# Fewer matmuls around the output projection of a cached decode step, and output weights of three head groups loaded in unequal parts

## The chip, the cores and the metric

The kernel runs on one core of one Trainium2 chip. The metric is the device time in microseconds (us) of one execution; a run gives the median of several. The inputs and the output are float32.

## The reference

Two attention blocks A and B read the same small input `x` (2 batches, 512 columns), each with its own key and value caches (2 batches, 32 heads, 4096 tokens, 128 per head) and weights, and a sigmoid gate mixes the two results. Cut to what matters:

```python
x = A_x                                              # (2, 1, 512)
g = sigmoid((x * gate_w).sum(-1, keepdims=True))
def block(x, k_cache, v_cache, wq, wo):
    q = (x @ wq).reshape(B, 1, 32, 128)               # one query row per batch and head
    scores = einsum("bhqd,bhkd->bhqk", q, k_cache) * 128 ** -0.5
    o = einsum("bhqk,bhkd->bhqd", softmax(scores), v_cache)
    return o.reshape(B, 1, 32 * 128) @ wo             # (2, 1, 512)
return g * block(A) + (1 - g) * block(B)
```

Each cache value is used once, so 570 MB come in from HBM and 4 KB go out.

## The kernel before, in words

A *group* is four heads of one network (8 groups in each of A and B); a *unit* `u` is a group and a batch, so there are 32 units, and two units in a row (b = 0 and 1) share a group. Each quarter of the 128 partitions holds one head of the unit, and each partition 128 tokens.

For a unit the keys come in two tiles of 4 MB (`kt`, three buffers), the values in one tile of 8 MB (`vt`, one buffer). For each group there is one tile of output weights (`wo`, 1 MB, two buffers): 128 rows of 8 KB, one for each partition. VectorE (DVE) multiplies the keys by the query and sums along the head (`scores`, L252 and L254), then finds the maximum (`soft`). ScalarE (ACT) makes the exponentials. TensorE (PE) multiplies them with the values (`values`, L275, 32 matmuls of 512 columns into four strips of 32 rows of one PSUM tile `vp`); ACT copies `vp` to `vs`; PE gathers the four heads (`gather_out`), DVE divides by the sums and applies the gate (`normalise`), PE deals the result over the partitions (`spread_out`, L326) and multiplies it with the output weights into `acc` (`project_out`, L336). A float32 matmul of the code stands twice in the trace as a weight load and a matmul.

The order is written out by hand: every engine runs its own instructions in the order of the code, and a loop over `u` works on the keys of unit u, the values of unit u - 1 and the output of the group that ended before that. All large loads are issued by SyncE (SP) from one queue, in the order of the list `order`; `pump` takes the next one as soon as the tile that it overwrites has been used. SP runs them in that order, so a load that waits holds back all loads behind it. Eight semaphores go round over the loads, so a load also waits for the one that had its semaphore before. The last unit's values come in pieces that get smaller (`load_v_half`), and the last group's output weights come last of all, in two pieces.

Of the kernel before, what the change touches and what calls it, by code (L numbers as in the profile page):

```python
# [13 lines left out]
P = 128  # L14
B = 2
# [11 lines left out]
KB = 3  # L27
VC = 4
NVC = NS // VC
NPR = 3  # L30
QT = 32
STRIPS = P // QT
OR = G * DH // P
EC = D // STRIPS
SCALE = DH ** -0.5
QUARTERS = [slice(j * PH, (j + 1) * PH) for j in range(G)]


@with_exitstack
def tile_gated_decode(ctx: ExitStack, tc: tile.TileContext, ins: dict, out: bass.AP):  # L40
# [52 lines left out]
    def load_wo(n, g):  # L93
        wo[n, g] = wpool.tile([P, OR, D], F32, name="wo")
        rows = ins[n + "_wo"][g * G * DH:(g + 1) * G * DH]
        if (n, g) != last:
            nc.sync.dma_start(wo[n, g], rows.rearrange("(p r) e -> p r e", p=P))
        else:

            t = rows.rearrange("(h p) e -> p h e", p=P)  # L100
            for i in range(0, G, 2):
                nc.sync.dma_start(wo[n, g][:, i:i + 2], t[:, i:i + 2])
# [35 lines left out]
    pump()  # L138


    consts.tile([P, 32], F32, name="gap")
    ident = consts.tile([P, P], F32)
    make_identity(nc, ident)
    ones = consts.tile([P, P], F32)
# [3 lines left out]
    for c in range(KC):  # L148
# [5 lines left out]
    nc.vector.memset(xs, 0.0)  # L154
    nc.vector.tensor_copy(xs[:, :, :B], cols_ps[:, :, :B])

    one = consts.tile([P, STRIPS, B, PH], F32)
    nc.vector.tensor_copy(
        one, ident.rearrange("p (s q) -> p s q", q=QT)[:, :, :B, None].to_broadcast([P, STRIPS, B, PH]))

    padded, sums, sums_of_values = [], [], []
    for i in range(NPR):
        t = consts.tile([P, NVC, G * VC], F32, name=f"pr{i}")
        nc.vector.memset(t, 0.0)
        padded.append(t)
    for i in range(2):
        t = ps.tile([P, VC * DH], F32, name=f"vp{i}", bufs=1)
        nc.vector.memset(t, 0.0)  # L170
        sums_of_values.append(t)

    outs = []
    for i in range(2):
        t = consts.tile([P, OR, QT], F32, name=f"on{i}")
        nc.vector.memset(t, 0.0)
        outs.append(t)
# [6 lines left out]
    pick = consts.tile([P, VC, G], F32)  # L184
    nc.vector.tensor_reduce(
        pick, ident.rearrange("p (s j a) -> p a j s", s=STRIPS, a=VC)[:, :, :G, :], axis=AX.X, op=ALU.add)

    picks = consts.tile([P, B, VC, B, G], F32)
    nc.vector.memset(picks, 0.0)
    for b in range(B):  # L190
        nc.vector.tensor_copy(picks[:, b, :, b, :], pick)

    qa, qrow = {}, {}

# [14 lines left out]
    def spread_queries(u):  # L209

        n, g, b = units[u]
        qp = ps.tile([P, DH], F32, name="qp", bufs=1)
        for j, quarter in enumerate(QUARTERS):
            nc.tensor.matmul(qp[quarter], one[:, g % STRIPS, b], qrow[n][:, g // STRIPS, j * DH:(j + 1) * DH],  # L214
                             start=True, stop=True)
        qs[u] = work.tile([P, DH], F32, name="q", bufs=3)
        nc.scalar.activation(qs[u], qp, AF.Copy)  # L217


    gate = {}  # L220
# [1 line left out]
    def make_gate():  # L222
# [12 lines left out]
        gate["last"] = consts.tile([P, B, G], F32, name="gate")  # L235
        nc.vector.tensor_copy(gate["last"], other[:, :, None].to_broadcast([P, B, G]))
        mine = consts.tile([B * G, B], F32, name="mine")
        nc.vector.tensor_reduce(mine, ident[:B * G, :B * G].rearrange("p (b h) -> p b h", b=B), axis=AX.X, op=ALU.add)
        for n, t in (("A", g), ("B", other)):
            m = consts.tile([B * G, B], F32, name="gm" + n)  # L240
            nc.vector.tensor_tensor(m, mine, t[:B * G], op=ALU.mult)
            gate[n] = consts.tile([B * G, 1], F32, name="gate" + n)
            nc.vector.tensor_reduce(gate[n], m, axis=AX.X, op=ALU.add)

    sc, pr, lp, vp, ot, ls, vs, on, rs, row, cp = ({} for _ in range(11))

    def scores(u, i, k):

# [7 lines left out]
    def soft(u):  # L256
        rm = work.tile([P, 1], F32, name="rm")
        nc.vector.tensor_reduce(rm, sc[u], axis=AX.X, op=ALU.max)  # L258

        across = work.tile([P, PH], F32, name="across")  # L260
        nc.vector.transpose(across, rm.to_broadcast([P, PH]))
        nm = work.tile([P, 1], F32, name="nm")
        nc.vector.tensor_reduce(nm, across, axis=AX.X, op=ALU.max, negate=True)  # L263
        n, g, b = units[u]
        pr[u], lp[u] = padded[u % NPR], sums[u // B % 3]
        for j, h in enumerate(QUARTERS):
            nc.scalar.activation(pr[u][h, :, j * VC:(j + 1) * VC], sc[u][h].rearrange("p (c a) -> p c a", a=VC),  # L267
                                 AF.Exp, bias=nm[h], accum_out=lp[u][h, b * G + j:b * G + j + 1])

    def values(u):  # L270
        vp[u] = sums_of_values[u % 2]
        for c in range(NVC):
            s = c % STRIPS
            t = vt[u][:, c * VC:(c + 1) * VC] if u in vt else vt[u, c * VC // NT][:, c * VC % NT:c * VC % NT + VC]
            nc.tensor.matmul(vp[u][s * QT:s * QT + G * VC], pr[u][:, c, :], t.rearrange("p a d -> p (a d)"),  # L275
                             start=c < STRIPS, stop=c >= NVC - STRIPS)
        vs[u] = work.tile([P, VC * DH], F32, name="vs")
        nc.scalar.activation(vs[u], vp[u], AF.Copy)  # L278

    def gather_out(u):  # L280
        n, g, b = units[u]
        if (n, g) == last:

            if b == 0:
                ot[n, g] = ps.tile([P, B, G], F32, name="ot", bufs=1)
            for a in range(VC):
                nc.tensor.matmul(ot[n, g][:, b], vs[u][:, a * DH:(a + 1) * DH], pick[:, a],  # L287
                                 start=a == 0, stop=a == VC - 1)
            return
        if b == 0:  # L290
            ot[n, g] = ps.tile([B * G, DH], F32, name="ot", bufs=1)
        for a in range(VC):
            nc.tensor.matmul(ot[n, g], picks[:, b, a].rearrange("p b j -> p (b j)"), vs[u][:, a * DH:(a + 1) * DH],  # L293
                             start=(b, a) == (0, 0), stop=(b, a) == (B - 1, VC - 1))

    def sum_of(n, g, u):

        if (n, g) == last:
            ls[n, g] = ps.tile([P, B * G], F32, name="small", bufs=1)
            nc.tensor.matmul(ls[n, g], ones, lp[u], start=True, stop=True)  # L300
        else:
            ls[n, g] = ps.tile([B * G, 1], F32, name="small", bufs=1)
            nc.tensor.matmul(ls[n, g], lp[u], ones[:, :1], start=True, stop=True)  # L303

    def invert(n, g):
        rs[n, g] = work.tile(ls[n, g].shape, F32, name="rsl" if (n, g) == last else "rs", bufs=1)
        nc.vector.reciprocal(rs[n, g], ls[n, g])
        by = gate["last"].rearrange("p b h -> p (b h)") if (n, g) == last else gate[n]
        nc.vector.tensor_tensor(rs[n, g], rs[n, g], by, op=ALU.mult)

    def normalise(n, g):
        on[n, g] = outs[g % 2]
        if (n, g) == last:
            nc.vector.tensor_tensor(on[n, g][:, :, :B].rearrange("d h b -> d b h"), ot[n, g],  # L314
                                    rs[n, g].rearrange("p (b h) -> p b h", b=B), op=ALU.mult)
            return
        row[n, g] = work.tile([B * G, DH], F32, name="row", bufs=1)
        nc.vector.tensor_scalar(row[n, g], ot[n, g], rs[n, g], None, op0=ALU.mult)  # L318

    def spread_out(n, g):  # L320


        cp[n, g] = ps.tile([P, OR, B], F32, name="small", bufs=1)
        for h in range(G):
            for r in range(OR):
                nc.tensor.matmul(cp[n, g][h * QT:(h + 1) * QT, r], row[n, g][:, r::OR], ident[:B * G, h:B * G:G],  # L326
                                 start=True, stop=True)
        nc.scalar.activation(on[n, g][:, :, :B], cp[n, g], AF.Copy)  # L328


    acc = ps.tile([P, EC], F32, name="acc", bufs=1)

    def project_out(n, g):
        for r in range(OR):
            for s in range(STRIPS):
                nc.tensor.matmul(acc[s * QT:(s + 1) * QT], on[n, g][:, r], wo[n, g][:, r, s * EC:(s + 1) * EC],  # L336
                                 start=(n, g, r) == ("A", 0, 0), stop=(n, g, r) == (*last, OR - 1))

    for c in range(KC):
        project("A", c)  # L340
# [5 lines left out]
    for u in range(NU + 2):  # L346
# [7 lines left out]
        if u + 1 < NU:  # L354
            spread_queries(u + 1)
        if ended and ended != last:
            spread_out(*ended)
        if ends:
            sum_of(*ends, v)
        if u < NU:  # L360
            scores(u, 0, 1)
            used("k", u, 0)
        if ends:
            invert(*ends)
        if 0 <= v < NU:
            values(v)
            used("v", v)
            gather_out(v)
        if ended:
            project_out(*ended)  # L370
            used("wo", *ended)
# [40 lines left out]
```

## Time and profile before

| | before |
|---|---|
| median of 3 runs (lowest to highest) | 1331.59 us (1331.37 to 1331.93) |
| profiled execution, its own time | 1331.76 us |
| its span in the profile | 1330.0 us |
| HBM read | 570.43 MB, 429 GB/s over the span |
| busy share of the span: PE, DVE, ACT | 29%, 87%, 7% |
| PE matmuls and weight loads | 3724 and 3724 |

The device time is 1.8 us longer than the span, which runs from the first to the last instruction. In the windows of the profile, PEclk is the clock that TensorE was granted as a share of full speed, and the DMA share is the mean busy share of the core's 16 DMA engines; a packet is counted where it starts, so in short windows the share can be a little over 1. In the list of queues, q1 is the queue of SP's loads, and q8 and q14 are those over which the engines' own instructions are fetched. A row of the chain of waits gives the start in us, the length in us, and what took the time.

### The profile page before, as it was taken

How to read it: one execution, taken by the hardware profiler on the slowest of the kernel's cores; microseconds unless marked ns; L12 is line 12 of the kernel's file. 1: busy time of each engine (PE TensorE's matmuls, PEld its weight loads, DVE VectorE, ACT ScalarE, POOL GpSimd, SP SyncE). 2: the span in 40 equal slices, each digit the busy share in tenths (PEclk: the TensorE clock that was granted, in tenths of full speed). 3: DMA queues.
4: the chain of work that ended last, by engine and by line, in shares of the span. 5: the costliest groups of instructions: out<-in, count | busy, mean ns of one | idle time of the engine just before them, and what ended most of it. 6: DMA issues, size and time to landing. Idle time of an engine off the chain costs nothing.

```text
span 1330.0 us, 8602 instructions
## 1 busy us (share of the span) xinstructions
PE 391.7 (29%) x3724; PEld 136.3 (10%) x3724; DVE 1157.8 (87%) x429; ACT 96.9 (7%) x341; POOL 0.7 (0%) x6
## 2 busy tenths in 40 slices
PE   4033123333213332152123332223332133332136
PEld 1000001101001110010001101011110011100012
DVE  2999999989989898938998989989899998989984
ACT  0000000000000000000000000000000000000000
POOL 0000000000000000000000000000000000000000
PEclk9566566765566666586576665666665566665669
DMA  9999999999999999999999999999999999999997
GB/s 410 442 433 417 438 427 447 428 428 433 432 443 428 436 427 432 431 443 423 437 433 441 428 427 435 432 436 436 436 429 429 432 433 445 434 419 434 429 436 315
DMA packets 18172, 570.99 MB, mean 429 GB/s; under 512 B 1995, under 2 KB 2003, under 8 KB 2774
## 3 DMA queue, kind: packets, MB, share of 16 engines
q1 hardware_dynamic: 18120, 570.44, 99.4%
q8 instruction: 29, 0.48, 0.1%
q14 instruction: 9, 0.07, 0.0%
q10 hardware_dynamic: 14, 0.01, 0.0%
HBM read 570.43 MB, written 0.00 MB: 429 GB/s over the span
## 4 chain that ended last, share of the span: by engine, by line
DMA 75%; PE 21%; DVE 3%; issue 0%; SPq 0%; ACT 0%; ACTq 0%; DVEq 0%
DMA vt<-in_A_v_cache_dram 38%; DMA vt<-in_B_v_cache_dram 30%; PE vp L275 20%; DMA kt<-in_B_k_cache_dram 3%; DMA kt<-in_B_v_cache_dram 2%; DMA kt<-in_A_wq_dram 2%; DVE sc L254 1%; DVE kt L252 1%; PE qa L201 1%; SPq L66 0%; PE acc L336 0%; ACT vs L278 0%; PE ot L287 0%; PE small L225 0%; PE ot L293 0%
## 5 line engine op out<-in xcount | busy, mean ns | idle before, releaser
L252 DVE TENSOR_TENSOR kt<-kt,q 128x4096 f32<-128x4096 f32 x128 | 565.1, 4415 | 120.0 <-DMA kt<-in_A_k_cache_dram 54.2
L254 DVE TENSOR_REDUCE sc<-kt 128x32 f32<-128x4096 f32 x128 | 565.8, 4420 | 4.4
L275 PE MATMUL vp<-vt,pr 128*16 128x512 f32 x1984 | 283.1, 734 | 709.3 <-DMA vt<-in_A_v_cache_dram 380.2
L275 PEld LDWEIGHTS vp<-vt,pr 128*16 128x16 f32 x1984 | 63.3, 113 | 903.7 <-issue 505.5
L278 ACT ACTIVATE vs<-vp 128x512 f32<-128x512 f32 x32 | 19.1, 597 | 961.9 <-PE vp L275 961.9
L326 PE MATMUL small<-ident,row 8*32 8x2 f32 x480 | 21.5, 197 | 160.5 <-DVE row L318 160.5
L267 ACT ACTIVATE pr<-sc,nm 32x128 f32<-32x128 f32 x128 | 51.0, 398 | 63.7 <-DVE nm L263 61.9
L293 PE MATMUL ot<-vs,picks 128*8 128x128 f32 x240 | 31.2, 273 | 23.3 <-ACT vs L278 23.3
L326 PEld LDWEIGHTS small<-ident,row 8*32 8x32 f32 x480 | 20.3, 149 | 164.6 <-DVE row L318 164.6
L293 PEld LDWEIGHTS ot<-vs,picks 128*8 128x8 f32 x240 | 19.1, 89 | 54.4 <-ACT vs L278 50.9
L201 PE MATMUL qa<-kt,xs 128*32 128x512 f32 x128 | 20.3, 787 | 13.1 <-DMA kt<-in_B_wq_dram 4.5
L267 ACT ACTIVATION_READ_ACCUMULATOR pr<-sc,nm 32x1 f32 x128 | 23.5, 184 | 0.0
L336 PE MATMUL acc<-wo,on 128*32 128x128 f32 x512 | 19.6, 275 | 0.3 <-DVE on L314 0.3
L214 PE MATMUL qp<-qrow,one 128*32 128x128 f32 x256 | 18.0, 278 | 0.4 <-ACT q L217 0.4
L336 PEld LDWEIGHTS acc<-wo,on 128*32 128x32 f32 x512 | 15.4, 109 | 0.4 <-DVE on L314 0.4
L229 DVE TENSOR_SCALAR ge<-ge 128x2 f32<-128x2 f32 x1 | 0.2, 169 | 16.4 <-ACT ge L228 16.4
L328 ACT ACTIVATE on<-small 128x8 f32<-128x8 f32 x15 | 2.7, 179 | 157.9 <-PE small L326 157.9
L314 DVE TENSOR_TENSOR on<-ot,rsl 128x8 f32<-128x8 f32 x1 | 0.2, 172 | 12.2 <-PE ot L287 12.2
L217 ACT ACTIVATE q<-qp 128x128 f32<-128x128 f32 x32 | 8.9, 278 | 17.6 <-PE small L303 17.0
L258 DVE TENSOR_REDUCE rm<-sc 128x1 f32<-128x128 f32 x32 | 9.2, 286 | 1.1
L214 PEld LDWEIGHTS qp<-qrow,one 128*32 128x32 f32 x256 | 9.8, 108 | 2.1 <-ACT qrow L207 0.8
L275 PE MATMUL vp<-kt,pr 128*16 128x512 f32 x64 | 8.7, 595 | 2.2 <-DMA kt<-in_B_v_cache_dram 2.2
(50 smaller groups left out, 52.6 us busy)
## 6 DMA issues: line engine op xcount, KB each, us to landing
kt<-in_B_k_cache_dram SPq DMA_DIRECT2D x32, 4096.0 KB, 37.2
kt<-in_A_k_cache_dram SPq DMA_DIRECT2D x31, 4096.0 KB, 34.5
kt<-in_A_wq_dram SPq DMA_DIRECT2D x2, 4096.0 KB, 21.2
wo<-in_A_wo_dram SPq DMA_DIRECT2D x8, 1024.0 KB, 32.0
kt<-in_B_wq_dram SPq DMA_DIRECT2D x2, 4096.0 KB, 35.9
vt<-in_B_v_cache_dram SPq DMA_DIRECT2D x2, 4096.0 KB, 27.2
wo<-in_B_wo_dram SPq DMA_DIRECT2D x7, 1024.0 KB, 31.3
kt<-in_B_v_cache_dram SPq DMA_DIRECT2D x3, 2048.0 KB
```

The costliest lines, as they stand in the source:

```text
L201: nc.tensor.matmul(qa[n, i // STRIPS][s * QT:(s + 1) * QT], xs[:, c], wq[n, c][:, i * G * DH:(i + 1) * G * DH], start=c == 0, stop=c == KC ...
L214: nc.tensor.matmul(qp[quarter], one[:, g % STRIPS, b], qrow[n][:, g // STRIPS, j * DH:(j + 1) * DH], start=True, stop=True)
L217: nc.scalar.activation(qs[u], qp, AF.Copy)
L252: nc.vector.tensor_tensor(t, t, qs[u][:, None, :].to_broadcast([P, NH, DH]), op=ALU.mult)
L254: nc.vector.tensor_reduce(sc[u][:, c:c + NH], t, axis=AX.X, op=ALU.add)
L258: nc.vector.tensor_reduce(rm, sc[u], axis=AX.X, op=ALU.max)
L267: nc.scalar.activation(pr[u][h, :, j * VC:(j + 1) * VC], sc[u][h].rearrange("p (c a) -> p c a", a=VC), AF.Exp, bias=nm[h], accum_out=lp[u] ...
L275: nc.tensor.matmul(vp[u][s * QT:s * QT + G * VC], pr[u][:, c, :], t.rearrange("p a d -> p (a d)"), start=c < STRIPS, stop=c >= NVC - STRIPS)
L278: nc.scalar.activation(vs[u], vp[u], AF.Copy)
L293: nc.tensor.matmul(ot[n, g], picks[:, b, a].rearrange("p b j -> p (b j)"), vs[u][:, a * DH:(a + 1) * DH], start=(b, a) == (0, 0), stop=(b, ...
L326: nc.tensor.matmul(cp[n, g][h * QT:(h + 1) * QT, r], row[n, g][:, r::OR], ident[:B * G, h:B * G:G], start=True, stop=True)
L336: nc.tensor.matmul(acc[s * QT:(s + 1) * QT], on[n, g][:, r], wo[n, g][:, r, s * EC:(s + 1) * EC], start=(n, g, r) == ("A", 0, 0), stop=(n, ...
```

## The change

The change has two parts.

The arithmetic around the values is laid out anew. Both batches of a group go into one `vp`: the exponentials stand in a tile that is zero for the other batch, so a matmul has 32 columns of weights where it had 16, and `vs` and the gather are done once for a group. The gather now gives its result with the head's 128 elements on the partitions (`pick`, 4 matmuls of 8 columns). Dealing it out takes 4 matmuls (`deal_out`) and two DVE operations (`keep_own`) where it took 16 small matmuls and an ACT copy; the projection takes 4 matmuls of 512 columns (into `most`, 2 partitions) where it took 16 of 128 columns; the query is spread by one matmul of 512 columns and four ACT copies where it took four matmuls and one copy. Only the last group keeps the old projection into `acc`; `take_most` adds what the other fifteen gave.

The output weights of groups 4, 5 and 6 of B are loaded in several transfers: the first 112 partitions, and then the last 16 in parts of 8, 8; of 7, 5, 3, 1; and of 6, 4, 4, 2.

```diff
+PARTS = {("B", 4): (112, 120), ("B", 5): (112, 119, 124, 127), ("B", 6): (112, 118, 122, 126)}
...
-            nc.sync.dma_start(wo[n, g], rows.rearrange("(p r) e -> p r e", p=P))
+            src = rows.rearrange("(p r) e -> p r e", p=P)
+            cuts = (0, *PARTS.get((n, g), ()), P)
+            for i, j in zip(cuts, cuts[1:]):
+                nc.sync.dma_start(wo[n, g][i:j], src[i:j])
...
     def spread_queries(u):
-        qp = ps.tile([P, DH], F32, name="qp", bufs=1)
+        qp = ps.tile([P, G, DH], F32, name="qp", bufs=1)
+        k = g % STRIPS * QT + b
+        nc.tensor.matmul(qp, ident[:, k:k + 1].to_broadcast([P, P]), qrow[n][:, g // STRIPS], start=True, stop=True)
...
-            nc.tensor.matmul(qp[quarter], one[:, g % STRIPS, b], qrow[n][:, g // STRIPS, j * DH:(j + 1) * DH],
-                             start=True, stop=True)
-        nc.scalar.activation(qs[u], qp, AF.Copy)
+            nc.scalar.activation(qs[u][quarter], qp[quarter, j], AF.Copy)
...
+    def gather_out(n, g):
+        vs[n, g] = work.tile([P, VC * DH], F32, name="vs", bufs=1)
+        nc.scalar.activation(vs[n, g], vp[n, g], AF.Copy)
+        ot[n, g] = ps.tile([P, B * G], F32, name="small", bufs=1)
+        for a in range(VC):
+            nc.tensor.matmul(ot[n, g], vs[n, g][:, a * DH:(a + 1) * DH], pick[:, a], start=a == 0, stop=a == VC - 1)
...
+    def deal_out(n, g):
+        cp[n, g] = ps.tile([P, OR, B, G], F32, name="small", bufs=1)
+        for r in range(OR):
+            nc.tensor.matmul(cp[n, g][:, r].rearrange("p b h -> p (b h)"), deal[:, r].rearrange("p g q -> p (g q)"),
+                             on[n, g], start=True, stop=True)
+    def keep_own(n, g):
+        t = work.tile([P, OR * B, G], F32, name="all", bufs=1)
+        nc.vector.tensor_tensor(t, cp[n, g].rearrange("p r b h -> p (r b) h"),
+                                own[:, None, :].to_broadcast([P, OR * B, G]), op=ALU.mult)
+        on[n, g] = work.tile([P, OR * B], F32, name="dealt")
+        nc.vector.tensor_reduce(on[n, g], t, axis=AX.X, op=ALU.add)
...
+            if (n, g) != last:
+                nc.tensor.matmul(most, on[n, g][:, r * B:(r + 1) * B], wo[n, g][:, r],
+                                 start=(n, g, r) == ("A", 0, 0), stop=(n, g, r) == ("B", NG - 2, OR - 1))
+                continue
...
+    def take_most():
+        kept = consts.tile([B, D], F32, name="kept")
+        nc.scalar.activation(kept, most, AF.Copy)
+        for s in range(STRIPS):
+            nc.tensor.matmul(acc[s * QT:(s + 1) * QT], ident[:B, :QT], kept[:, s * EC:(s + 1) * EC],
+                             start=True, stop=False)
```

On PE, the rows of one group (from the query of the unit to the projection of the group before; the last number of a row is a count). Before:

```order
L214 MATMUL qp<-qrow,one 32x128 x4
L303 MATMUL small<-ones,lp_121 8x1
L275 MATMUL vp_113<-vt,pr_105 16x512 x32
L293 MATMUL ot<-vs,picks 8x128 x4
L214 MATMUL qp<-qrow,one 32x128 x4
L326 MATMUL small<-ident,row 32x2 x16
L275 MATMUL vp_111<-vt,pr_107 16x512 x32
L293 MATMUL ot<-vs,picks 8x128 x4
L336 MATMUL acc<-wo,on_117 32x128 x16
```

And after:

```order
L208 MATMUL qp<-qrow,ident 128x512
L279 MATMUL small<-lp_111,ones 128x8
L264 MATMUL vp<-vt,pr_105 32x512 x32
L274 MATMUL small<-pick,vs 128x8 x4
L208 MATMUL qp<-qrow,ident 128x512
L300 MATMUL small<-on,deal 128x8 x4
L264 MATMUL vp<-vt,pr_103 32x512 x32
L318 MATMUL most<-wo,dealt 2x512 x4
```

These are 113 matmuls of the code before and 79 after; the matmuls on the values keep their number and place, and the rest shrinks.

On SP, the loads around the output weights of group 5 of B. Before:

```order
L66 DMA vt<-in_B_v_cache_dram 128x16384
L97 DMA wo<-in_B_wo_dram 128x2048
L66 DMA kt<-in_B_k_cache_dram 128x8192 x2
L66 DMA vt<-in_B_v_cache_dram 128x16384
L66 DMA kt<-in_B_k_cache_dram 128x8192 x2
```

And after:

```order
L67 DMA vt<-in_B_v_cache_dram 128x16384
L101 DMA wo<-in_B_wo_dram 112x2048
L101 DMA wo<-in_B_wo_dram 7x2048
L101 DMA wo<-in_B_wo_dram 5x2048
L101 DMA wo<-in_B_wo_dram 3x2048
L101 DMA wo<-in_B_wo_dram 1x2048
L67 DMA kt<-in_B_k_cache_dram 128x8192 x2
L67 DMA vt<-in_B_v_cache_dram 128x16384
L67 DMA kt<-in_B_k_cache_dram 128x8192 x2
```

Five transfers stand where one stood, ahead of the next keys; no load changes its turn.

On PE, the end of the program, from the projection of the last group but one. Before:

```order
L336 MATMUL acc<-wo,on_115 32x128 x16
L300 MATMUL small<-lp_119,ones 128x8
L275 MATMUL vp_113<-kt,pr_107 16x512 x32
L287 MATMUL ot<-pick,vs 128x4 x4
L336 MATMUL acc<-wo,on_117 32x128 x16
```

And after:

```order
L318 MATMUL most<-wo,dealt 2x512 x4
L279 MATMUL small<-lp_109,ones 128x8
L329 MATMUL acc<-kept,ident 32x128 x4
L264 MATMUL vp<-kt,pr_105 32x512 x32
L274 MATMUL small<-pick,vs 128x8 x4
L322 MATMUL acc<-wo,wide 32x128 x16
```

The four matmuls of `take_most` have come in ahead of the last unit's values; what follows the values has the same count.

More of the change, by code (lines that the diff above doesn't have):

```diff
@@ L138, in tile_gated_decode @@
     pump()
-    consts.tile([P, 32], F32, name="gap")
+    consts.tile([P, 104], F32, name="gap")
     ident = consts.tile([P, P], F32)
@@ L155, in tile_gated_decode @@
     nc.vector.tensor_copy(xs[:, :, :B], cols_ps[:, :, :B])
[L157 to L165, printed above, removed]
+    padded, sums = [], []
+    for i in range(B):
+        t = consts.tile([P, NVC, B, G * VC], F32, name=f"pr{i}")
         nc.vector.memset(t, 0.0)
         padded.append(t)
[L168 to L177, printed above, removed]
+    wide = consts.tile([P, G, QT], F32)
+    nc.vector.memset(wide, 0.0)
     for i in range(3):
@@ L233, in make_gate @@
         nc.vector.tensor_scalar(other, g, -1.0, 1.0, op0=ALU.mult, op1=ALU.add)
[L235 to L238, printed above, removed]
         for n, t in (("A", g), ("B", other)):
[L240 to L245, printed above, removed]
+            gate[n] = consts.tile([P, B, G], F32, name="gate" + n)
+            nc.vector.tensor_copy(gate[n], t[:, :, None].to_broadcast([P, B, G]))
+    sc, lp, vp, ot, ls, vs, on, rs, cp = ({} for _ in range(9))
     def scores(u, i, k):
@@ L296, in sum_of @@
[L296 to L309, printed above, removed]
@@ new lines, in sum_of, with invert, normalise @@
+    def sum_of(n, g, u):
+        ls[n, g] = ps.tile([P, B * G], F32, name="small", bufs=1)
+        nc.tensor.matmul(ls[n, g], ones, lp[u], start=True, stop=True)
+    def invert(n, g):
+        rs[n, g] = work.tile([P, B * G], F32, name="rs", bufs=1)
+        nc.vector.reciprocal(rs[n, g], ls[n, g])
+        nc.vector.tensor_tensor(rs[n, g], rs[n, g], gate[n].rearrange("p b h -> p (b h)"), op=ALU.mult)
+    def normalise(n, g):
+        if (n, g) == last:
+            nc.vector.tensor_tensor(wide[:, :, :B].rearrange("d h b -> d b h"),
+                                    ot[n, g].rearrange("p (b h) -> p b h", b=B),
@@ L315, in normalise @@
                                     rs[n, g].rearrange("p (b h) -> p b h", b=B), op=ALU.mult)
             return
[L317 to L328, printed above, removed]
+        on[n, g] = work.tile([P, B * G], F32, name="on", bufs=1)
@@ L331, in tile_gated_decode @@
+    most = ps.tile([B, D], F32, name="most", bufs=1)
     acc = ps.tile([P, EC], F32, name="acc", bufs=1)
@@ L362, in tile_gated_decode @@
             used("k", u, 0)
+        if ended and ended != last:
+            keep_own(*ended)
         if ends:
             invert(*ends)
+        if u == NU:
+            take_most()
         if 0 <= v < NU:
@@ L367, in tile_gated_decode @@
             used("v", v)
-            gather_out(v)
+        if ends:
+            gather_out(*ends)
         if ended:
```

56 lines of the change are left out of this document (20 added, 36 removed).

## The prediction

> **What bounds the kernel now.** I read the page first (busy shares, queues, the chain), then the chain in order of time, then the last microseconds in windows of 1 us.
>
> ```profile
> PE 391.7 (29%) x3724; PEld 136.3 (10%) x3724; DVE 1157.8 (87%) x429; ACT 96.9 (7%) x341; POOL 0.7 (0%) x6
> q1 hardware_dynamic: 18120, 570.44, 99.4%
> q8 instruction: 29, 0.48, 0.1%
> HBM read 570.43 MB, written 0.00 MB: 429 GB/s over the span
> L252 DVE TENSOR_TENSOR kt<-kt,q 128x4096 f32<-128x4096 f32 x128 | 565.1, 4415 | 120.0 <-DMA kt<-in_A_k_cache_dram 54.2
> ```
>
> SP's loads keep the 16 DMA engines busy for 99.4% of the span; the busiest computing engine, DVE, is idle for 120 us ahead of this line alone, 54.2 of them waiting for the keys of A. So the bytes bound the kernel, and a third of the matmuls is off the path as work. What can move the time is how the bytes end.
>
> ```profile
> 1234.10 40.06 DMA kt<-in_B_k_cache_dram
> ...
> 1293.52 29.18 DMA kt<-in_B_v_cache_dram
> 1322.75 1.06 PE vp L275 x4
> ...
> 1327.01 0.29 DVE total L386
> ```
>
> The chain of waits ends in a load: the last piece of values lands at 1322.70 (1293.52 + 29.18), and copy, gather, projection and output follow it to 1330.0.
>
> ```profile
> 1318.00:1319.00 1.00, 1.00 (x12) 0.23 (x8) 0.00 (x0) 0.00 (x0) 0.00 (x0) 1.00 0.98 397
> 1319.00:1320.00 1.00, 0.72 (x8) 0.00 (x0) 0.00 (x0) 0.00 (x0) 0.00 (x0) 1.00 0.67 272
> 1320.00:1321.00 1.00, 0.70 (x8) 0.13 (x8) 0.00 (x0) 0.00 (x0) 0.00 (x0) 1.00 0.59 240
> 1321.00:1322.00 1.00, 0.81 (x8) 0.12 (x4) 0.00 (x0) 0.00 (x0) 0.00 (x0) 1.00 0.60 231
> 1322.00:1323.00 1.00, 0.83 (x6) 0.12 (x4) 0.00 (x0) 0.00 (x0) 0.00 (x0) 1.00 0.53 193
> 1323.00:1324.00 1.00, 0.79 (x4) 0.00 (x0) 0.00 (x0) 0.11 (x1) 0.00 (x0) 1.00 0.39 152
> 1324.00:1325.00 1.00, 0.46 (x4) 0.46 (x5) 0.00 (x0) 0.49 (x1) 0.00 (x0) 1.00 0.23 88
> 1325.00:1326.00 1.00, 0.74 (x11) 0.65 (x14) 0.17 (x1) 0.00 (x0) 0.00 (x0) 1.00 0.00 0
> ```
>
> The last but one column is the DMA share. It doesn't fall at once. Up to 1319 all 16 engines work; then the share is 0.67, so five of them have run out; at 1322 to 1323 about half are left (0.53); after 1325 none. If a load of 128 partitions gives every engine the same bytes, the late engines have had something else to do. From 1319 to 1325 the missing shares sum to 0.33 + 0.41 + 0.40 + 0.47 + 0.61 + 0.77 = 2.99 us. That is what perfect balance would give, and every load's landing waits for the latest engine.
>
> **Where the lateness comes from.**
>
> ```profile
> q8 instruction: 1, 0.02, 0.6%
> q8 instruction: 1, 0.02, 0.3%
> ```
>
> These are from the queue lists of the windows 80 to 90 and 1310 to 1330 us. In the first, one instruction packet took 0.6% of 16 engines x 10 us, 0.96 us of one engine; the second shows that one of the 29 came in the last 20 us. The page has 29 such packets, 0.48 MB; PE ran 3724 + 3724 = 7448 instructions, 257 for each packet, so PE is being fed in blocks. The last half of the engines (0.53 + 0.39 + 0.23 = 1.15 us of 16 engines after 1322, 18.4 engine-us, so 2.3 us each) end at 1324.3 on average, 5.2 us after the first five. If 28 packets went to these eight by turns, 3.5 each, one costs 1.49 us, the packet and a gap about it. If they went over all 16, the step between 1319 and 1322 would not be there. I take 1.4 to 1.5.
>
> [...]
>
> **The change part by part.**
>
> *Fewer PE instructions.* The order gives 1864 matmuls of the code before and 1348 after (16 groups of 79, 72 to project the queries and set up, 12 more in the last group); at four instructions each, 5392, and 5392 / 257 = 21 packets, 20 before the end where there were 28. Over eight engines by turns the latest has three where it had four: 1 x 1.45 = **-1.4 us** on the path. Bounds: 0, if the packets have no part in the lateness; two packets fewer on the latest, -2.9.
>
> *Parts of the output weights.*
>
> ```profile
> wo<-in_B_wo_dram SPq DMA_DIRECT2D x7, 1024.0 KB, 31.3
> ```
>
> A load is 128 rows of 8 KB, 1.05 MB at 429 GB/s = 2.44 us, and eight rows for each engine: 0.306 us a row. 112 partitions are seven rows an engine; the other 16 rows go in parts of at most eight, so on at most eight engines if one row is one piece. An engine that gets none is spared one row in each of three loads: 3 x 0.306 = **-0.9 us**. The first engine gets up to 10 rows (2 + 4 + 4) instead of 3, +2.1 us, and 2.1 us on an engine that ran out at 1319 is covered by the 3.5 us that the latest then still has. No row shows which engines a small part takes. If they are the late ones, it is +2.1 instead. I take -0.9: late and early engines are two halves of eight, and the half that parts are dealt to is one or the other; the range keeps both ends. [...]
>
> The ten more transfers cost SP turns.
>
> ```profile
> 1233.25 0.44 SPq L97
> SPq L102 <- DMA vt<-in_B_v_cache_dram: 8.8, 1, 8.8
> ```
>
> An issue takes 0.44 us, so the next keys go out 0.9 to 1.8 us later; the load above took 31.3 us from issue to landing, 2.4 of them its own, so some 29 us of queue cover it. The 8.8 us show the eight semaphores at work: the last load waited for the one eight before it. With five parts in a row the load eight before is at least a unit's keys old (some 30 us), and has landed. 0.
>
> *The new order of the output.*
>
> ```profile
> L318 DVE TENSOR_SCALAR row<-ot,rs 8x128 f32<-8x128 f32 x15 | 4.9, 329 | 0.0
> 1262.04 8.83 PE L275 MATMUL vp<-vt,pr 128*16 128x512 f32 x64 [26.22 <-DMA vt<-in_B_v_cache_dram]
> ```
>
> DVE gets three operations of 8 or 32 columns for a group where it had one of 128 (L318, 0.33): at most +0.7 us for two units, beside its idle time: 0. `keep_own` waits for four matmuls that are issued a `scores` of 8.8 us (two of 4.4) earlier; without that cover DVE would lose their 1 us a group. The projection grows from 16 matmuls of 128 columns side by side to four of 512 one after the other: at 0.45 us a pass (below) 8 x 0.45 = 3.6 us, behind the values and ahead of the next unit's, for which PE has waited 26.22 us. 0.
>
> At the end the cover is thin:
>
> ```profile
> 1312.93 3.63 PE L275 MATMUL vp<-kt,pr 128*16 128x512 f32 x32
> 1317.81 1.91 PE L275 MATMUL vp<-kt,pr 128*16 128x512 f32 x16 [1.25 <-DMA kt<-in_B_v_cache_dram]
> 1320.30 1.05 PE L275 MATMUL vp<-kt,pr 128*16 128x512 f32 x8 [0.58 <-DMA kt<-in_B_v_cache_dram]
> 1323.89 0.60 ACT L278 ACTIVATE vs<-vp 128x512 f32<-128x512 f32 x1 [11.33 <-PE vp L275]
> ```
>
> 32 matmuls in four strips take 3.63 us, 0.45 for a pass of 512 columns. The last unit's values start at 1312.93 and then wait for loads, 1.25 us and 0.58 us. `take_most` puts an ACT copy of 512 columns (0.60) and four matmuls (at most 0.45) ahead of them, with DVE's 0.7 at most 1.75 us. The two waits together are 1.83. The keys before it land earlier by the same as the values, so the order of the two keeps. 0, up to +0.5. After the last load the counts on PE, ACT and DVE are the same.
>
> *The start.*
>
> ```profile
> 0.74 0.88 SPq L90 DMA_DIRECT2D kt<-in_A_wq_dram  x2
> 27.63 0.43 PE L214 MATMUL qp<-qrow,one 128*32 128x128 f32 x8
> 28.33 0.27 ACT L217 ACTIVATE q<-qp 128x128 f32<-128x128 f32 x1
> 29.07 0.17 ACT L228 ACTIVATE ge<-small 128x2 f32<-128x2 f32 x1 [0.47 <-PE small L225]
> 30.64 4.40 DVE L252 TENSOR_TENSOR kt<-kt,q 128x4096 f32<-128x4096 f32 x1
> 48.31 0.33 SPq L66
> ```
>
> At 48.31 SP issues keys that had waited for DVE's first two scores. Ahead of them stood five tiles of 4.19 MB, 48.9 us at 429 GB/s, issued from 0.74 on and so begun between 1 and 2: the queue was some 2 us from empty. So here the path runs through the first query. Its matmul goes from 0.43 to two passes of 0.45 or more (+0.5), three more copies come in ahead of `ge` on ACT (0.2 to 0.27 each, partly beside PE's work on the gate), and `ge` comes 0.7 us later; the gate loses four small DVE operations of the 1.4 us between `ge` and L252, 0.6. Net **+0.1**, between -0.3 and +0.7.
>
> **The sum.** -1.4 - 0.9 + 0.1 = -2.2 or -2.3 us against the profiled execution's 1331.76 us (span 1330.0): 1329.5. That execution stands 0.17 above the median, so I predict 1329.3 us, -0.17%. About 0.2%, 2.7 us, is what a measurement of this kernel tells from no change, so the forecast falls just inside it.
>
> **The rivals.**
> - *Full balance.* The latest engine loses two packets, or its load falls to the mean: 2.99 us of missing shares and 8 packets x 1.45 / 16 = 0.7 make 3.7 us, 1327.9. For it: five engines idle for 6 us have room for all rows. Against: 20 packets on eight engines leave three on some.
> - *The parts go to the late engines, or to one that is late for another reason* (there are engines that ran out between 1319 and 1322, late by 1 to 3 us without being of the last eight). Then 2.1 us eat the gain: 1329.9 to 1332.4. The rows show no number of an engine.
> [...]
> - *Slower: the parts collide.* All loads of before but a few tiny ones write 128 partitions, eight an engine; a load of 112 may give engines rows that two must write by the same way. If the 16 last rows go four deep (4 x 0.306 instead of 0.306, +0.9) and the seven at half speed (+2.1), three loads cost 9.2 us on every engine: 1331.6 - 1.4 + 9.2 = 1339.4; a quarter of that, 2.3, is the point from which it decides, and 5 us from which it is slower by 0.2%. No row speaks for or against it. [...]
>
> **How the numbers follow.** Main case 0.52, about 1328.4 to 1330.3; full balance 0.14; no gain or little (wrong engines, hidden fetch, tail or start) 0.19; collision 0.15, most of it over 1332. Faster by over 0.2% (under 1328.9): all of full balance and four tenths of the main case, 0.35. Slower by over 0.2% (over 1334.3): 0.12 of the collision. Same: 0.53. The range leaves out what lies under 1328.0 (0.07) and the collisions over 1333.0 (0.13). The main case's own range is 1328.4 to 1330.3.
>
> **What would show it.** Packets on q8: 21. The fall of the DMA share at the end: the missing shares under 2 us, and from full to none in under 4.5 us. The last values landing 2.2 us earlier, near 1320.5, with the same 7.3 us behind. SP's keys of 48.31 within 0.7 us. Wrong would be: a DMA rate that dips near 1262 us (1233.25 and 29 of queue) and one and two groups earlier, where the parts are loaded (collision); a late engine that the tail shows beyond 4.5 us (wrong engines); PE without a wait between the last values' pieces (the tail has become computing).

## The result, and the profile after

The changed kernel takes 1347.40 us (1346.37 to 1352.97) against 1331.59: a ratio of 1.0122 [1.0111, 1.0133], slower by 16 us. The forecast was 1329.3. The profiled execution took 1346.37 us, its span is 1344.6.

On the page after, these rows answer to those shown of before (busy us, share and instructions of PE; then what the DMA engines moved in 40 slices of 33.6 us; then packets, MB and share by queue, and the bytes read):

```profile
PE 452.8 (34%) x2692; PEld 151.0 (11%) x2692; DVE 1159.6 (86%) x449; ACT 110.8 (8%) x407; POOL 0.7 (0%) x6
GB/s 406 437 435 423 435 435 446 431 423 431 435 435 435 436 435 426 431 443 422 436 434 434 438 433 437 423 431 430 438 437 435 424 370 445 433 356 429 369 427 324
q1 hardware_dynamic: 18168, 570.44, 99.5%
q8 instruction: 21, 0.34, 0.1%
HBM read 570.43 MB, written 0.00 MB: 424 GB/s over the span
```

Before, what the DMA engines moved (40 slices of 33.25 us) was:

```profile
GB/s 410 442 433 417 438 427 447 428 428 433 432 443 428 436 427 432 431 443 423 437 433 441 428 427 435 432 436 436 436 429 429 432 433 445 434 419 434 429 436 315
```

PE has 28% fewer matmuls but more busy time, 452.8 us against 391.7, which is still far from the span. The bytes are the same and q1 is as busy as before, but the rate over the span has fallen from 429 to 424 GB/s. The loss isn't spread out: three slices, the 33rd, 36th and 38th, stand at 370, 356 and 369 GB/s, and the others near those of before. The busy share of 99.5% doesn't show it; the windows below have 0.98 at 230 GB/s and 0.96 at 413.

The chain of waits shows the same as time (start, length, what): the start of the values of three units, before

```profile
1062.49 9.66 PE vp L275 x64
1142.26 9.03 PE vp L275 x64
1223.50 9.37 PE vp L275 x64
```

and after, with the last piece of all:

```profile
1061.17 9.79 PE vp L264 x64
1146.93 9.57 PE vp L264 x64
1231.87 9.77 PE vp L264 x64
1337.21 1.08 PE vp L264 x4
```

At 1061 us the changed kernel is 1.3 us ahead. One dip later it is 4.7 behind, then 8.4, and at the last piece (1322.75 before) 14.5. So 15.8 us are lost in three steps of 6.0, 3.7 and 6.1, 5.3 on average.

Windows of 10 us on the first dip, after, and the middle one of before. The columns are the length, then the busy time and the count of PE, of its weight loads, of DVE, ACT and POOL, then PEclk, the DMA share and GB/s:

```profile
1085.00:1095.00 10.00, 0.00 (x0) 0.00 (x0) 9.93 (x5) 0.00 (x0) 0.00 (x0) 0.50 0.97 419
1095.00:1105.00 10.00, 0.28 (x4) 0.20 (x8) 9.97 (x3) 0.00 (x0) 0.00 (x0) 0.50 0.98 230
1105.00:1115.00 10.00, 9.21 (x73) 2.95 (x66) 2.03 (x4) 1.61 (x6) 0.00 (x0) 0.87 0.98 392
```

```profile
1095.00:1105.00 10.00, 3.97 (x20) 0.83 (x24) 9.97 (x3) 0.00 (x0) 0.00 (x0) 0.50 0.96 413
```

For more than 10 us the engines are busy and move little more than half of what they move elsewhere. In windows of 2 us the rate stays between 123 and 356 GB/s from 1094 to 1108, 3.60 MB in all. The output weights in parts are at most 1.05 MB of these, so some 2.5 MB of the loads around them are slowed too.

### The profile page after: what moved, and what is told of

It reads as the page before. It is cut to its first block, busy times and chain, and to the rows that moved or that the text cites. A ratio compares the mean times of both kernels' runs of the same rounds, so it can differ in the third digit from the quotient of the medians.

```text
span 1344.6 us, 6698 instructions
## 1 busy us (share of the span) xinstructions
PE 452.8 (34%) x2692; PEld 151.0 (11%) x2692; DVE 1159.6 (86%) x449; ACT 110.8 (8%) x407; POOL 0.7 (0%) x6
## 3 DMA queue, kind: packets, MB, share of 16 engines
q1 hardware_dynamic: 18168, 570.44, 99.5%
## 4 chain that ended last, share of the span: by engine, by line
DMA 75%; PE 21%; DVE 3%; issue 0%; SPq 0%; ACT 0%; DVEq 0%; ACTq 0%
DMA vt<-in_A_v_cache_dram 37%; DMA vt<-in_B_v_cache_dram 31%; PE vp L264 20%; DMA kt<-in_B_k_cache_dram 3%; DMA kt<-in_B_v_cache_dram 2%; DMA kt<-in_A_wq_dram 2%; DVE sc L241 1%; DVE kt L239 1%; PE qa L195 1%; PE most L318 0%; SPq L67 0%; SPq L101 0%; PE acc L322 0%; PE small L274 0%; ACT q L211 0%
## 5 line engine op out<-in xcount | busy, mean ns | idle before, releaser
L264 PE MATMUL vp<-vt,pr 128*32 128x512 f32 x1984 | 287.3, 743 | 684.9 <-DMA vt<-in_A_v_cache_dram 360.7
L264 PEld LDWEIGHTS vp<-vt,pr 128*32 128x32 f32 x1984 | 73.9, 133 | 874.5 <-issue 491.4
L300 PE MATMUL small<-on,deal 128*128 128x8 f32 x120 | 28.1, 364 | 151.3 <-DVE on L293 151.3
L318 PE MATMUL most<-wo,dealt 128*2 128x512 f32 x120 | 53.9, 592 | 0.0
L300 PEld LDWEIGHTS small<-on,deal 128*128 128x128 f32 x120 | 26.7, 327 | 163.0 <-DVE on L293 163.0
L211 ACT ACTIVATE q<-qp 32x128 f32<-32x128 f32 x128 | 34.3, 268 | 74.2 <-PE qp L208 72.4
L208 PE MATMUL qp<-qrow,ident 128*128 128x512 f32 x64 | 36.6, 654 | 1.6 <-ACT q L211 1.6
L195 PE MATMUL qa<-kt,xs 128*32 128x512 f32 x128 | 21.3, 799 | 12.4 <-DMA kt<-in_A_wq_dram 7.7
L274 PE MATMUL small<-pick,vs 128*128 128x8 f32 x128 | 16.9, 259 | 12.5 <-ACT vs L271 12.5
L274 PEld LDWEIGHTS small<-pick,vs 128*128 128x128 f32 x128 | 15.5, 191 | 27.0 <-ACT vs L271 27.0
L223 DVE TENSOR_SCALAR ge<-ge 128x2 f32<-128x2 f32 x1 | 0.2, 170 | 17.8 <-ACT ge L222 17.8
L318 PEld LDWEIGHTS most<-wo,dealt 128*2 128x2 f32 x120 | 10.2, 85 | 40.6 <-issue 40.3
```

The source lines that it names most:

```text
L195: nc.tensor.matmul(qa[n, i // STRIPS][s * QT:(s + 1) * QT], xs[:, c], wq[n, c][:, i * G * DH:(i + 1) * G * DH], start=c == 0, stop=c == KC ...
L208: nc.tensor.matmul(qp, ident[:, k:k + 1].to_broadcast([P, P]), qrow[n][:, g // STRIPS], start=True, stop=True)
L211: nc.scalar.activation(qs[u][quarter], qp[quarter, j], AF.Copy)
L264: nc.tensor.matmul(vp[n, g][s * QT:(s + 1) * QT], padded[b][:, c].rearrange("p b m -> p (b m)"), t.rearrange("p a d -> p (a d)"), start=b ...
L274: nc.tensor.matmul(ot[n, g], vs[n, g][:, a * DH:(a + 1) * DH], pick[:, a], start=a == 0, stop=a == VC - 1)
L300: nc.tensor.matmul(cp[n, g][:, r].rearrange("p b h -> p (b h)"), deal[:, r].rearrange("p g q -> p (g q)"), on[n, g], start=True, stop=True)
```

## The experiments

All edits are to the changed kernel unless another is named; the kernel before had medians of 1332.01 to 1332.12 us beside them. A run given with a single time was executed once. The changed kernel's own five executions lie between 1346.37 and 1352.97 us, so differences of a few us between single runs that show the dips say little.

**Which half of the change costs.** The first run takes the parts out of the change, the second puts them alone into the kernel before:

```diff
-PARTS = {("B", 4): (112, 120), ("B", 5): (112, 119, 124, 127), ("B", 6): (112, 118, 122, 126)}
+PARTS = {}
```

> The changed kernel with the output weights of all groups loaded whole, as before; the new arithmetic alone. Theory (the parts cost it all, the fewer PE instructions gain what the prediction gave): 21 packets on q8, the latest DMA engine has three of them instead of four, 1331.6 - 1.4 = 1330.2 us. Rival (the new arithmetic costs time somewhere): 1333 us or more, up to 1347. Rival (instruction packets do not matter): 1331.6.

Measured: 1330.81 us (1329.95 to 1332.06), ratio 0.9989 [0.998, 0.9998]. The end in windows of 1 us:

```profile
1319.00:1320.00 1.00, 0.12 (x4) 0.12 (x8) 0.00 (x0) 0.00 (x0) 0.00 (x0) 1.00 0.90 360
1320.00:1321.00 1.00, 0.95 (x8) 0.04 (x5) 0.00 (x0) 0.00 (x0) 0.00 (x0) 1.00 0.69 274
1321.00:1322.00 1.00, 0.90 (x4) 0.14 (x4) 0.00 (x0) 0.00 (x0) 0.00 (x0) 1.00 0.63 244
1322.00:1323.00 1.00, 0.82 (x6) 0.14 (x4) 0.00 (x0) 0.00 (x0) 0.00 (x0) 1.00 0.52 203
1323.00:1324.00 1.00, 0.38 (x2) 0.00 (x0) 0.00 (x0) 0.51 (x1) 0.00 (x0) 1.00 0.27 102
1324.00:1325.00 1.00, 0.86 (x8) 0.86 (x8) 0.00 (x0) 0.09 (x1) 0.00 (x0) 1.00 0.03 12
```

The missing shares from 1319 to 1324 are 0.10 + 0.31 + 0.37 + 0.48 + 0.73 = 1.99 us, where they were 2.99. By the medians (1330.81 against 1332.01 beside it) the rest of the change is worth about 1.2 us, and the parts cost 1347.40 - 1330.81 = 16.6. This profiled execution was the slowest of the eleven, 1332.06: at its end the granted clock fell to 0.50 and the last projection took 1.81 us, where it took 1.12 before.

The edit of the second run, in the kernel before:

```diff
+PARTS = {("B", 4): (112, 120), ("B", 5): (112, 119, 124, 127), ("B", 6): (112, 118, 122, 126)}
...
-            nc.sync.dma_start(wo[n, g], rows.rearrange("(p r) e -> p r e", p=P))
+            src = rows.rearrange("(p r) e -> p r e", p=P)
+            cuts = (0, *PARTS.get((n, g), ()), P)
+            for i, j in zip(cuts, cuts[1:]):
+                nc.sync.dma_start(wo[n, g][i:j], src[i:j])
```

> The kernel before with the loads of the output weights of groups 4, 5 and 6 of B cut as in the change; nothing else. Theory (the parts collide, whatever PE does): the excess of the changed kernel's packets, 15.7 us, comes here too: 1331.6 + 15.7 = 1347.3 us, with the DMA rate near 230 GB/s for some 10 us at each of the three loads. Rival (parts hurt only together with the new arithmetic): 1331 to 1333 us.

Measured: 1351.0 us, with 248 GB/s from 1095 to 1105 us, where the kernel before has 413. The parts alone cost 19 us, 6.3 a load, with nothing else changed; that lies within the spread of the changed kernel.

**Is it the small parts?** One cut at 112 for each of the three loads, or one at 64:

```diff
+PARTS = {("B", g): (112,) for g in (4, 5, 6)}     # the third run
+PARTS = {("B", g): (64,) for g in (4, 5, 6)}      # the fourth
```

> The changed kernel with the same three loads cut once, at partition 112: parts of 112 and of 16 partitions. Theory (what costs is that a part's rows fall to other DMA engines than those of a whole load): seven rows an engine are off already, so at least 10 of the 15.7 us stay: 1340 to 1346 us. Rival (the small parts of 1 to 8 partitions cost it, because a few engines carry all their rows): 16 rows go to 16 engines, one each, and nothing is left: 1330.2 us.

Measured: 1347.32 us, and the same three dips:

```profile
GB/s 405 434 435 422 435 433 445 433 427 427 436 434 439 429 435 427 433 442 427 427 436 434 440 431 435 425 436 431 438 436 427 432 361 441 436 357 428 368 427 324
```

> The changed kernel with the same three loads cut once, at partition 64: two parts of 64. Every DMA engine gets four rows of each part, so rows are even and no part is small. Theory (rows fall to other engines than in a whole load, or to half of the ways into memory): at least the 2.4 us of a load is spent twice, +2.4 to +5.5 us a load: 1337 to 1346 us. Rival (uneven rows or small parts cost): 1330.2 us.

Measured: 1353.48 us. Neither the parts of 1 to 8 rows nor uneven rows for each engine are the cause: one cut at 112 costs what the change costs, and two equal halves cost at least as much, 22.7 us, 7.6 a load (0.5 us above the slowest execution of the changed kernel).

**Loads alone.** Nothing is left but loads of 4.19 MB into one tile, whole and in parts by turns, each waiting for the one before:

```python
for i, j in zip(cuts, cuts[1:]):
    nc.sync.dma_start(t[i:j], r[i:j])     # (0,112,128), (0,64,128), 32s, 16s, (0,112,119,124,127,128)
for i in range(2):
    nc.sync.dma_start(big[i::2], r[i::2]) # even partitions, odd partitions
```

> No attention and no output, only loads of one tile of 4.19 MB (128 partitions, 32 KB each) from the keys, one after the other: whole, and in between cut at 112; at 64; at 32, 64, 96; in eight parts of 16; at 112, 119, 124, 127; and the even and the odd partitions apart. Each cut load waits for the whole one ahead of it, so its time stands alone. Theory (rows of a part go through fewer or shared ways into memory): whole 9.7 us and 2 for the issue; halves and quarters 1.5 to 2 times 9.7 us; parts of 16 some 4 times; even and odd partitions close to whole, as they keep all ways. Rival (a part costs a fixed time for itself): all cuts of two parts cost the same, eight parts the most by the number alone, some 2 us a part. Rival (parts are only slow beside other traffic): all cuts near 9.7 us.

Measured, in the chain of waits (start, length): whole and 112/16; whole and 64/64; whole and eight of 16; whole and even/odd (the rows between these are left out). A load in parts lasts from the end of the row ahead of it to the end of its own, since its row begins with its last part.

```profile
0.73 12.39 DMA big<-in_A_k_cache_dram
13.53 20.00 DMA big<-in_A_k_cache_dram
33.60 12.29 DMA big<-in_A_k_cache_dram
46.49 22.02 DMA big<-in_A_k_cache_dram
103.29 12.13 DMA big<-in_A_k_cache_dram
118.56 35.43 DMA big<-in_A_k_cache_dram
194.33 12.35 DMA big<-in_A_k_cache_dram
207.23 11.79 DMA big<-in_A_k_cache_dram
```

Whole 12.1 to 12.4 us; 112/16 20.4; 64/64 22.6; four of 32, by the same view, 22.4; eight of 16 38.6; 112/7/5/3/1 27.8; even and odd partitions 12.3. Two transfers of 64 partitions thus take nearly twice the time of a whole load or no longer than it, depending only on *which* 64. Less some 2.6 us that a whole load takes beyond its 9.8 us of bytes at 429 GB/s, halves and quarters take about 2.0 times as long for their bytes as a whole load, and eighths (16 partitions) 3.7 times; even and odd partitions are at full rate. At the rate of the whole load 112 partitions would take 8.6 us, and 16 at that of the eighths 4.5, together 13.1 (an estimate from these rows); 20.4 - 2.6 = 17.8 is measured, so 112/16 is slower than the rates of its parts would make it.

**Does it hold in the full kernel?** The three loads in even and odd partitions; and in as many transfers as in the change (three, five, five), each of 128 partitions and cut along the row:

```diff
+            if n == "B" and g in (4, 5, 6):
+                for i in range(2):
+                    nc.sync.dma_start(wo[n, g][i::2], src[i::2])
```
```diff
+PIECES = {("B", 4): (0, 1, 2, 4), ("B", 5): (0, 1, 2, 3, 4), ("B", 6): (0, 1, 2, 3, 4)}
...
-                nc.sync.dma_start(wo[n, g][i:j], src[i:j])
+                nc.sync.dma_start(wo[n, g][:, i:j], src[:, i:j])
```

> The changed kernel, with the three loads of output weights each in two parts again, but one part takes the even partitions and one the odd ones, not the lower and the upper 64. If a load is slow because a range of neighbouring partitions uses only a part of the ways into the SBUF, both parts use all ways, and nothing is lost: 1330.8 us (1330 to 1332), no dip of the rate. Rival: it is the number of partitions in a transfer, or that two transfers write one tile, which costs: then as with two halves, 1349 to 1354 us, with dips near 1100, 1180 and 1262.

> The changed kernel, with the three loads cut into as many transfers as in the change (three, five, five), but along the row, so that each writes all 128 partitions with pieces of 2 to 4 KB. If the partitions of a transfer decide, nothing is lost: 1330.8 us (1330 to 1332), no dip of the rate. Rival: the number of transfers, their issues or their smaller packets cost: 1335 us or more, with the loss in the two groups of five parts larger than in the one of three.

Measured: 1332.07 and 1330.90 us, one execution each, without a dip. The window that moved 230 GB/s in the changed kernel, with even and odd partitions:

```profile
1095.00:1105.00 10.00, 3.48 (x20) 0.85 (x24) 9.97 (x3) 0.00 (x0) 0.00 (x0) 0.50 0.96 413
```

So neither the number of transfers, nor 64 partitions in a transfer, nor SP's additional issues cost anything that shows; ranges of neighbouring partitions do. In all these runs a range of partitions is also a range of neighbouring rows in HBM, so a cause on the reading side is not excluded by a run of its own. Halves and quarters, with different ranges in HBM, cost the same alone (22.6 and 22.4 us); that the cause lies on the side of the SBUF was the author's estimate and was not shown.

**A miss: eight parts of 16.**

```diff
+PARTS = {("B", g): tuple(range(16, 128, 16)) for g in (4, 5, 6)}
```

> The changed kernel with the three loads of output weights in eight parts of 16 partitions each; one row for each of the 16 DMA engines in every part. Theory (ways into memory: 16 partitions have a quarter of them): a load of 2.4 us takes 9.8 us or more, at least +7.3 a load, 1352 us or more, above the cut at 64 (1353) if that lost by half the ways alone. Rival (rows away from their own engine run at half speed whatever the cut): 5 to 6 us a load as with the other cuts, 1346 to 1349 us.

Measured: 1345.35 us, under both expectations. SP's rows in the timeline and the window of the dip tell that this run tests something else as well:

```profile
1069.53 34.84 SPq L101 DMA_DIRECT2D wo<-in_B_wo_dram  x8
```
```profile
1095.00:1105.00 10.00, 0.91 (x8) 0.26 (x12) 9.97 (x3) 0.00 (x0) 0.00 (x0) 0.50 0.60 163
```

With eight transfers in a row the eight semaphores are used up: SP stands at L101 until 1104, and the next keys are issued only then. The engines run dry (share 0.60), so part of the loss is idle time, and the parts have no load behind them to disturb. How the two share the 14.5 us was not taken apart.

**Why 5 us and not 2?** Alone, 112/16 loses 8 us on 4.19 MB, which would be 2 us on 1.05 MB (an estimate), but in the full kernel such a load of 1.05 MB loses 5.3. The next run puts 1.05 MB of output weights, whole or in parts, between two whole loads of 4.19 MB, with nothing in the queue before, and the one after it makes half of the engines late first:

```python
for i in range(lag):                      # 0, 1 or 3; only in the second of the two
    nc.sync.dma_start(lags[i][0:32:4], vrows[...])   # 8 partitions of 32 KB
for s in cuts:
    nc.sync.dma_start(mid[s], wsrc[k * P:(k + 1) * P][s])
```

> Loads alone, everything else is left out. Seven times: a whole load of 4.19 MB, then 1.05 MB of output weights in the parts named, then another whole load of 4.19 MB, with nothing in the queue before, so that the engines are in step. Whole: 21.8 us of bytes and some 2.6 us fixed, 24.4. If only the ways of each part count, and parts don't overlap with their neighbours: 112/16 +2.0 us, 64/64 +2.5, eight of 16 +7, 112/7/5/3/1 +3.9, even/odd 0, whole again 0. If a part also slows the whole loads ahead of it and behind it (as in the full kernel, where 64/64 lost 5.6 to 7.7 us and eight of 16 lost 3): 64/64 and 112/16 +5 or more, eight of 16 under that.

Measured, in the chain (each row ends with the landing of its group's second whole load; the first three groups are whole, 112/16 and 64/64; the rows between these are left out):

```profile
1.65 23.50 DMA big<-in_A_k_cache_dram
26.49 25.06 DMA big<-in_A_k_cache_dram
53.18 25.05 DMA big<-in_A_k_cache_dram
```

From one landing to the next (25.15, 51.55, 78.23), against 24.3 for the whole one at the end: 112/16 +2.1, 64/64 +2.4; by the same rows 112/7/5/3/1 +4.1 and even/odd +0.1. In step, the parts cost what the expectation had scaled from the loads alone. (Eight of 16 again held up SP, +4.5, and isn't used.)

> Loads alone again, everything else is left out. Between the first whole load and the 1.05 MB of output weights now come none, one or three small loads of 8 partitions of 32 KB, which make eight of the engines 1.2 or 3.6 us late. Controls with a whole load: about 24.4, 25.6 and 28.0 us. Theory (the price grows when engines are out of step, since those that are still in a neighbouring load then write by the same ways as those in the parts): with three small loads 112/16 costs 4 to 6 us more than its control, 64/64 5 to 7, even/odd nothing; with one, 112/16 2.5 to 4; with none 2.0 as before. Rival (being out of step doesn't matter, the rest of the 5 us comes from the full kernel's work beside the loads): 112/16 +2.0 and 64/64 +2.3 against the control, whatever the lateness.

Measured, in the same view, again without the rows between; the groups are whole with no small loads ahead; with three of them whole, 112/16, 64/64, even/odd; with one of them whole, 112/16; and 112/16 with none:

```profile
1.65 23.37 DMA big<-in_A_k_cache_dram
28.06 24.82 DMA big<-in_A_k_cache_dram
56.34 28.27 DMA big<-in_A_k_cache_dram
88.31 31.48 DMA big<-in_A_k_cache_dram
123.60 24.04 DMA big<-in_A_k_cache_dram
149.31 23.72 DMA big<-in_A_k_cache_dram
175.22 26.42 DMA big<-in_A_k_cache_dram
202.99 24.73 DMA big<-in_A_k_cache_dram
```

From landing to landing: controls 24.3, 27.86 and 25.4 us, so the late engines are 3.5 and 1.1 us late. That they are eight, the packets of the queue agree with: the 3768 add up if a load makes one for each of its rows and one more for each engine that it uses, 8 and 8 for a small load and 128 and 16 for a whole one. 112/16 costs 26.1 - 24.3 = 1.8 with all in step, 28.6 - 25.4 = 3.2 with 1.1 us of lateness, and 31.73 - 27.86 = 3.9 with 3.5; 64/64 costs 35.18 - 27.86 = 7.3 where it cost 2.4; even/odd nothing. So lateness raises the price, with no computing beside: the rival falls. 112/16 stays a little under the 4 to 6 that were expected, and 64/64 a little over its 5 to 7. How late the engines are at the three loads of the full kernel was not measured, so that lateness makes the 5.3 to 5.5 us there is argued; at 3.5 us late, 1.4 to 1.6 of them are not accounted for.

**What the fewer matmuls are worth.** Dummy matmuls in `deal_out` of the kernel without parts bring the PE instructions back: 34 for each group make about as many as before, 102 far more.

```diff
+        for _ in range(34):               # 102 in the other
+            nc.tensor.matmul(cp[n, g][:QT, 0].rearrange("p b h -> p (b h)"), deal[:, 0, 0], on[n, g],
+                             start=True, stop=True)
```

> The same with 34 more matmuls a group instead of 102: as many PE instructions as the kernel before, 29 packets. Theory: four packets on the latest engine again, back to the time before, 1331.6 us, 1.4 above the kernel without parts. Rival: 1330.2 us.

Measured: 1331.74 us (1331.32 to 1333.21), ratio 0.9998 [0.9989, 1.0007], with 29 packets on q8 by its 7432 instructions, at 257 a packet. The end, from 1321 on:

```profile
1321.00:1322.00 1.00, 0.84 (x8) 0.14 (x4) 0.00 (x0) 0.00 (x0) 0.00 (x0) 1.00 0.58 231
1322.00:1323.00 1.00, 0.83 (x6) 0.14 (x4) 0.00 (x0) 0.00 (x0) 0.00 (x0) 1.00 0.54 209
1323.00:1324.00 1.00, 0.67 (x4) 0.00 (x0) 0.00 (x0) 0.22 (x1) 0.00 (x0) 1.00 0.36 137
1324.00:1325.00 1.00, 0.57 (x5) 0.57 (x6) 0.00 (x0) 0.38 (x1) 0.00 (x0) 1.00 0.21 80
```

With 0.70 and 0.64 ahead of them, the missing shares are 2.97 us, those of before (2.99). Instructions that compute nothing bring the old tail back.

> The new arithmetic without parts, and in each of the 15 groups that are dealt out 102 matmuls more on PE (32 columns of weights, 8 of data) that write what the first dealing matmul writes again; they stand where PE waits for values in any case. They bring PE from 5392 to about 11500 instructions, so 45 packets on q8 instead of 21. Theory (each packet makes one DMA engine late by 1.45 us, eight engines take turns): 44 before the end, six on the latest where there were three, 1330.2 + 4.35 = 1334.5 us, and a tail in which the missing DMA shares sum to 4 us or more. Rival (packets are free, PE work off the path is free): 1330.2 us and a tail as without them.

Measured: 1337.63 us, ratio 1.0046 [1.0032, 1.006], with 45 packets by its 11512 instructions. The tail grows as expected: from 1322 to 1326 the share stands at 0.50 and 0.51, eight engines, and 4.5 us are missing in all. But the time misses, since something else happened too:

```profile
1320.83 8.85 PE vp L264 x64
```

The dummies outlast the scores that cover them, the last values come late, and 64 matmuls run in one piece on the chain where two waits had been. The run confirms the tail and can't price it.

**The start.** The last run without parts computes the gate behind the first scores:

```diff
-    make_gate()
...
+        if u == 0:
+            make_gate()
```

> The changed kernel without the parts, and the gate of the two networks computed behind the first scores of unit 0 instead of ahead of them, so that DVE begins the first product some 2 us earlier. If the start is on the path (SP's issue at 48 us waits for DVE's first scores while the queue is nearly empty), the time is 0.2 to 0.5 us under that of the kernel without parts, about 1330.4 us. Rival: the queue still holds enough there, and it is 1330.8 like the kernel without parts. Against the kernel before: 1.2 to 1.7 us faster.

Measured: 1330.87 us (1330.34 to 1331.94), ratio 0.9991 [0.9982, 1.0]: the same as without the edit. SP's issue that waits for the first scores came at 48.03 us, against 48.45 in the changed kernel, so the edit saved 0.4 us there and not 2, and the time alone can't tell. Other runs moved this issue further. With 102 dummies it came at 46.98; without parts, where the projection of A's queries took 6.57 us against 5.09 in the changed kernel, it came at 50.02. That projection follows the granted clock: in the changed kernel it ran 12 matmuls in the 2.10 us from 22.9 on, at 0.50, and 16 in the 1.50 us from 26.0 on, at 1.00. The next values landed between 80.63 and 81.74 us in these runs, where the kernel before had 48.31 and 80.92. So an issue 3.0 us later (50.02 against 46.98) brought the landing 1.1 us later, and the start is on the path at most in part.

## Why the prediction was wrong

**The bound was right.** The bytes set the time, and fewer matmuls gained nothing as work.

**The instruction packets were right, as far as the runs can tell.** 21 packets came, as worked out. The term was -1.4 us. The kernel without parts gained 1.2 (by its interval 0.3 to 2.7), and giving the instructions back took 0.9 of it away. The missing shares at the end came under 2 us (1.82 in the changed kernel from 1334 to 1339, 1.99 without parts), as forecast; but the fall from full to none still took about 5 us (1319 to 1324), not under 4.5, and without parts the last values landed at 1322.28 in the profiled execution, not near 1320.5. The "hidden fetch" of the chances falls: dummies restore the tail, 2.97 us of missing shares against 1.99 without them.

**The parts of the output weights are the step that failed.** The prediction took -0.9 us from "112 partitions are seven rows an engine", as if a load cost an engine its own bytes and nothing else. Measured is +15.8 by the chain, +16.6 by the medians. Its upper bound, +2.1, was a matter of one engine's rows as well, so the true cost lay outside both ends. Whether a saving of 0.9 us is hidden in it can't be seen.

**The rival had the sign of what happened but not its size, nor its chance.** "The parts collide" put a dip of the rate near 1262 us and in the two groups ahead, and there it came: 284 GB/s from 1262 to 1272, 230 and 233 in the groups ahead. Its price was 3.06 us a load, 1339.4 in all, from 16 rows that go four deep and seven at half speed. No run shows these terms; the loads alone show 20.4 us for 112/16 against 12.1 to 12.4 for a whole load, and 2.0 times the time for halves and quarters, 3.7 for eighths. The price counted only the parts' own rows. In the first dip some 2.5 MB of the neighbouring loads are slowed as well, and the stream of loads shows that a load in parts costs 1.8 to 2.4 us with the engines in step, under that price, and 3.2 to 7.3 us out of step. The prediction's own tail rows had the engines out of step by 5 us, and it used them only to hide 2.1 us in. Its chance of 0.15 was argued from "No row speaks for or against it".

**What cost nothing, as said.** SP's five issues took 1.8 us in a row ahead of the keys, and three or five transfers along the row lost nothing. The start came at 48.45, +0.14 us (forecast +0.1), but the runs under "The start" show the path through it at most in part. The new projection cost what was taken:

```profile
L318 PE MATMUL most<-wo,dealt 128*2 128x512 f32 x120 | 53.9, 592 | 0.0
```

One pass of 512 columns lasts 0.59 us from its start to its end, but passes overlap: the 120 take 53.9 us of busy time, 0.45 a pass and 3.6 us a group, as forecast. The tail of the changed kernel has the 7.3 us of before behind the last landing (1337.17 to the end at 1344.6, 7.4).

**One sign of being wrong came from the parts, not from the new order.** In the changed kernel PE runs all of the last unit's values without a wait:

```profile
1328.34 9.92 PE L264 MATMUL vp<-kt,pr 128*32 128x512 f32 x64
```

The granted clock there was 0.50 from 1330 to 1332. The chain still ends in the landing at 1337.17, and without parts PE waits again for these loads, up to 1.11 us. So the cover that was thin was used up in this execution, but not by `take_most` alone.

## What to carry to other kernels

Before cutting a load into ranges of neighbouring partitions, time the cut load beside the whole one: cut along the row, or dealt alternately over the partitions, a load lost nothing that shows here (1330.90 and 1332.07 us against 1330.81); with a range cut off, the rate of all 16 engines fell to 230 GB/s, for the neighbouring loads in the queue too. Count the bytes moved (GB/s in the slices), not the busy share, to see it. And a rival that no row refutes deserves a price that includes what stands next to it in the queue.

## What the runs showed of the hardware that was not expected

- Two transfers of 64 partitions take 22.6 us as halves and 12.3 us as even and odd partitions, for the same 4.19 MB.
- Such a load costs more the further the engines are out of step: 64/64 of 1.05 MB 2.4 us in step, 7.3 with eight engines 3.5 us late; 112/16 1.8, 3.2 and 3.9 with 0, 1.1 and 3.5 us. In the full kernel it was 7.6 and 5.5. The kernel before with 29 instruction packets lost 6.3 us to each load in parts in its one execution, the changed one with 21 lost 5.3 to 5.5; the changed kernel's own executions spread over 6.6 us, so this says nothing of the packets.
- The pace ahead of the start went with the granted clock: in the changed kernel the projection of A's queries ran 12 matmuls in 2.10 us at 0.50 and 16 in 1.50 us at 1.00. It took 5.09 us there and 6.57 without parts, and SP's issue behind the first scores came at 48.45 and 50.02 us.
- What is open: how late the engines are at the three loads of the full kernel; why 112/16 takes longer alone (17.8 us) than the 13.1 estimated from the rates of a whole load and of eighths; and whether a range of partitions is slow by its place in the SBUF or by its rows in HBM.
